# The bias stage of an attention and mixture-of-experts kernel gets its own division of PSUM

## The chip, the cores and the metric

One core of a Trainium2 chip runs the whole program. The metric is the device time of one execution in microseconds; lower is better. The kernel before takes 603.62 us, the median of three runs (601.79 to 604.7).

## The reference

An attention layer whose scores carry a computed bias, followed by a mixture of experts with one expert per token. B, H, S, D = 4, 8, 576, 64; the bias net has 32 hidden units; the experts have D = 512, F = 1024, E = 8.

```python
scores = scale * np.matmul(q, k.transpose(0, 1, 3, 2))
x = (psi_rel / psi_i)[..., None]             # 576 x 576 positions
h = np.maximum(x @ w1 + b1, 0.0)             # 32 hidden units
bias = h @ w2                                # one bias per head
attn = softmax(scores + bias.transpose(2, 0, 1)[None])
x = np.matmul(attn, v)                       # as 2304 tokens x 512
# each token goes to its best expert e:
out[mask] = gate * eom * (np.maximum(x[mask] @ w1[e], 0.0) @ w2[e])
```

## The kernel before, in words

The program is written out in a fixed order: each engine executes its instructions in the order in which the Python code emits them, and waits only on semaphores. It has three parts.

**The stage of the bias** (the loop `for r16 in range(36)`) builds the bias tables of all heads. A step, called a bias row here, covers 16 query positions. `emit_hid` writes four tiles of hidden units (128x576), each by VectorE (L725) or ScalarE (L723); the string `ON_ACT` has one digit for each row that says how many of the four ScalarE takes. `emit_bias` multiplies them with the second layer on TensorE (16 matmuls, L736) into a tile `pb` of two PSUM banks. ScalarE scales and copies it out (L740) into one of four staging rows `evh`, `evl`, and SyncE's queue sends the row to the bias table in SBUF (L746; in the last four rows L749, two DMAs each). A staging row is written again four bias rows later, when its DMA has landed. The hidden tiles are emitted two rows ahead and have three buffers.

Between the rows stands work of the first pairs of heads, placed by the table `BEGIN`: `l` is the six loads of keys and queries of pair 1 (`emit_load`), `v` the load of the values of pair 0 (`emit_load_v`), `k0` to `k2` and `K0` to `K2` are the transposes of keys and queries of pairs 0 and 1 (`emit_kq`: three transposes on TensorE, L809, a rounding copy by ScalarE, L812, called cast here, and the rest by VectorE, L814, called split here), and `s00`, `s10`, `s01`, `s11` are scores of pair 0, one head each (`emit_s`: TensorE L832, then VectorE adds the bias and finds the row's extreme, L844, then ScalarE's exponential, L849). What `BEGIN` names for a row starts on TensorE behind that row; its second half is emitted one row later, behind the next hidden tiles.

**The pairs of heads.** Behind the loop the pool of the stage is closed, GpSimd clears some tiles in its place (L976), and 16 pairs of heads follow in the order of the strings `FIRST`, `ORDER`, `LAST`, `END`. In them `s` is the products of a score tile, `m` its softmax, `t` transposes of the exponentials (L885, copied out at L889), `a` the product with the values (L917), `l` and `v` the loads of later pairs, `h` and `k` their transposes, `z` GpSimd's copies (L820) that build the query tile of the fifth block, which `s4` reads. A `+` means the next pair. On SyncE's queue the weights of the gate (L965) stand between the last bias rows and the loads of pair 2 (`l++`). The first `t` also makes GpSimd copy values (L802).

**The experts** follow and are bound by TensorE.

PSUM has eight banks. `ps_t` holds three places of one bank for all transposes, `ps_s` two places of two banks, which bias rows and scores share, and `ps_a` one bank for the product with the values.

Of the kernel before, what the change touches and what calls it, by code (L numbers as in the profile page):

```python
# [9 lines left out]
F32 = mybir.dt.float32  # L10
# [8 lines left out]
PSUM = bass.MemoryType.PSUM  # L19
# [30 lines left out]
)  # L50

FIRST = (
    "l++ t04d s2 t03a m2 t02d z t00a s3 m3 v+ s4 t01a m4 "
)

LAST = (
# [7 lines left out]
)  # L64

BEGIN = {
    3: "k0", 4: "k1", 5: "k2 l", 13: "K0", 16: "K1", 17: "s00", 20: "K2",
    22: "s10 s01", 32: "s11", 35: "v",
}

ON_ACT = "210210000111121212102110310010201111"

SLOT_WORK = (
# [8 lines left out]
def _first_row(r16):  # L82

    qb, g = divmod(r16, 8)
    return qb * 128 + (g if qb == 4 else g // 2 + 64 * (g % 2))
# [48 lines left out]
def attention_moe_kernel(  # L134
# [26 lines left out]
    xt_p = ctx.enter_context(tc.tile_pool(name="xt", bufs=3))  # L161
    x_p = ctx.enter_context(tc.tile_pool(name="x", bufs=2))
    st_p = ctx.enter_context(tc.tile_pool(name="st", bufs=4))
    ps_t = ctx.enter_context(tc.tile_pool(name="ps_t", bufs=3, space=PSUM))
    x_dram = dram.tile([NTOK, DM], F32, name="x_dram")

    n_kept = _WHERE["psi"][0]
# [14 lines left out]
    V.memset(gate, 0.0)  # L182

    def psum_t():
        return ps_t.tile([128, 512], F32, name="pt", tag="t")

    def over(ap, shape):
        return ap.rearrange("p (o e) -> p o e", o=1).to_broadcast(shape)
# [66 lines left out]
    def route_group(part):  # L255
# [4 lines left out]
        t0, nt = ((0, NTA), (NTA, NT - NTA))[part]  # L260
        ts = slice(t0, t0 + nt)
        pr = psum_t()
        rest = pm[:, t0 + 1:t0 + nt, :]
        n8 = nt * 8
# [119 lines left out]
        for u in range(nt // 5):  # L384
# [24 lines left out]
            yield  # L409
            yield  # L410
            pi = psum_t()
            for i in range(2):
                for t in range(5):
# [259 lines left out]
    with ExitStack() as actx:  # L673
        pool = lambda name, bufs, **kw: actx.enter_context(tc.tile_pool(name=name, bufs=bufs, **kw))
        kq = pool("kq", 1)
        ps_s = pool("ps_s", 2, space=PSUM)
        ps_a = pool("ps_a", 1, space=PSUM)


        bctx = ExitStack()  # L680
        e_p = pool("e", 1)
        e_all = [e_p.tile([128, 2, S], F32, name=f"e{i}") for i in range(4)]
        hb = bctx.enter_context(tc.tile_pool(name="hb", bufs=3))
# [30 lines left out]
        def emit_hid(r16):  # L714
            hid = hb.tile([128, 3, S], F32, name="hid", tag="hid")
            hid3 = xt_p.tile([128, S], F32, name="hid3", tag="xt0", bufs=4)
            for t in range(4):
# [3 lines left out]
                to = hid3 if t == 3 else hid[:, t, :]  # L721
                if t >= 4 - int(ON_ACT[r16]):
                    nc.scalar.activation(out=to, in_=src, func=ACTF.Relu, bias=bc[:, r:r + 1])  # L723
# [6 lines left out]

        def emit_bias(r16, hids):
            ev = evs[r16 // 2 % 2][:, r16 % 2, :]
            pb = ps_s.tile([128, 2, 512], F32, name="pb", tag="s")
            for c in range(2):
                for t in range(4):
                    nc.tensor.matmul(  # L736
                        pb[32 * t:32 * t + 32, c, 0:288], lhsT=w2f, rhs=hids[t][:, c * 288:c * 288 + 288],
                        start=True, stop=True,
                    )
            nc.scalar.activation(  # L740
                out=ev.rearrange("p (a j) -> p a j", a=2), in_=pb[:, :, 0:288], func=ACTF.Copy,
                scale=cinv[:, r16:r16 + 1],
            )
            p0 = _first_row(r16) % 128
            if r16 < 32:
                nc.sync.dma_start(out=bias[r16 // 8][p0:p0 + 61:4], in_=ev)  # L746
            else:
                for hl in range(2):
                    nc.sync.dma_start(  # L749
                        out=bias[4][hl * 64 + p0:hl * 64 + p0 + 61:4],  # L750
                        in_=ev.rearrange("(n t) j -> t n j", t=2)[hl]
                    )
# [71 lines left out]
        def products(b, pr, qb, heads, outs):  # L824

            high, low = (t[(b * NPAIR + pr) % 2] for t in (high2, low2))
            for c in range(2):
                for i, (t, keys) in enumerate(((0, high), (0, low), (1, high))):
                    qs = (high, low)[t]
                    for hl in heads:  # L830
                        p = slice(hl * 64, hl * 64 + 64) if qb < 4 else slice(0, 128)
                        nc.tensor.matmul(  # L832
                            outs[hl][:, c, 0:288],
                            lhsT=qs[p, S + 64 + qb * 128:S + 192 + qb * 128] if qb < 4 else q4[:, t, :],
                            rhs=keys[p, c * 288:c * 288 + 288], start=i == 0, stop=i == 2,
                        )
# [4 lines left out]
        def softmax_rows(e, ps, bias_ap, sum_ap):  # L841
            nm = st_p.tile([128, 1], F32, name="nm", tag="nm")
            n = e.shape[-1] // 2
            V.tensor_tensor_reduce(  # L844
                out=e.rearrange("p (a j) -> p a j", a=2), in0=ps[:, :, 0:n],
                in1=bias_ap.rearrange("p (a j) -> p a j", a=2),
                scale=-0.125, scalar=3.0e38, op0=ALU.add, op1=ALU.min, accum_out=nm,
            )
            nc.scalar.activation(out=e, in_=e, func=ACTF.Exp, scale=-1.0, bias=nm, accum_out=sum_ap)  # L849

        def emit_s(b, pr, qb, heads=(0, 1)):
            if b not in sums_t:
                sums_t[b] = st_p.tile([128, 4, H], F32, name="sums", tag="sums", bufs=2)
                sums4_t[b] = st_p.tile([128, NPAIR], F32, name="sums4", tag="sums4", bufs=2)
            if qb == 4:
                e = e_t[b, pr, 4] = e4[0]
                ps = ps_s.tile([128, 2, 512], F32, name="ps", tag="s")
                products(b, pr, qb, (0,), [ps])
                yield
                softmax_rows(e, ps, bias[4][:, pr, :], sums4_t[b][:, pr:pr + 1])  # L860
                return
            e_t[b, pr, qb] = e_all[qb]
            ps = {hl: ps_s.tile([128, 2, 512], F32, name="ps", tag="s") for hl in heads}
            products(b, pr, qb, heads, ps)
            yield
            for hl in heads:
                h = 2 * pr + hl
                softmax_rows(e_t[b, pr, qb][:, hl, :], ps[hl], bias[qb][:, h, :], sums_t[b][:, qb, h:h + 1])
# [69 lines left out]
        def finish(g):  # L938
            for _ in g:
                pass  # L940
# [19 lines left out]
        for g in halfway:  # L960
            finish(g)
        bctx.close()
        for hl in range(2):
            for i, w in enumerate((wg, wog)):
                nc.sync.dma_start(  # L965
                    out=wgb[hl * 64:hl * 64 + 64, :, hl * 16 + i * 8:hl * 16 + i * 8 + 8],
                    in_=w.rearrange("(a t d) e -> t d a e", t=2, d=64)[hl],
                )
# [23 lines left out]
        for n in range(len(pairs) + 1):  # L992
            for op in orders.get(n, ORDER).split():
                name = op.rstrip("+-")
# [24 lines left out]
                elif name[0] in "mh":  # L1019
                    finish(late.pop({"m": "s", "h": "k"}[name[0]] + name[1]))  # L1020
                    if name[0] == "m" and m == len(pairs) - 1:
# [3 lines left out]
                        if i == 2:  # L1025
                            t = biasp.tile([128, 4, 4, CH], F32R, name="x", tag="bias2")
# [22 lines left out]
    with ExitStack() as ctx:  # L1049
# [8 lines left out]
        hh, hl = ([t[:, i, :] for i in range(8)] for t in (hh_all, hl_all))  # L1058
# [190 lines left out]
```

## Time and profile before

| | |
|---|---|
| median of 3 runs | 603.62 us (601.79 to 604.7) |
| the profiled execution's own time | 601.0 us |
| its span, first to last instruction | 599.2 us |
| TensorE busy (matmul) | 565.7 us, 94% |
| VectorE busy | 395.6 us, 66% |
| ScalarE busy | 374.6 us, 63% |
| GpSimd busy | 106.2 us, 18% |
| mean granted clock of TensorE | 0.988 |

The profile records one execution, and its rows add up to the span. Times in a row are counted from the span's start. A busy TensorE has its matmuls pipelined, so a busy share alone says little; what counts is in which stretch it stands idle and for whom. An instruction's duration overlaps the next one's on the same engine by some 0.1 us, so the cost of one in a series is the distance of two starts.

### The profile page before, as it was taken

The numbers are of one execution on the slowest core, as the hardware profiler recorded it, in microseconds if no ns is written. First come the engines' busy times: TensorE is split into PE (matmuls) and PEld (weight loads), VectorE is DVE, ScalarE is ACT, GpSimd is POOL, SyncE is SP. The second block draws the span as 40 slices with busy tenths as digits, with TensorE's granted clock in tenths as the row PEclk, the third lists the DMA queues.
The fourth block names the chain that finished last, engine by engine and source line by source line (L and its number), as shares of the span: only waits on it lengthen the run. The fifth ranks groups of instructions, "written<-read, shape, count | busy, mean of one in ns | idle before, by whom it ended". The sixth has DMA issues, their size and how long they took to land.

```text
span 599.2 us, 13978 instructions
## 1 busy us (share of the span) xinstructions
PE 565.7 (94%) x5294; PEld 471.1 (79%) x5294; DVE 395.6 (66%) x936; ACT 374.6 (63%) x812; POOL 106.2 (18%) x220
## 2 busy tenths in 40 slices
PE   4888789999999999999999999999999999999993
PEld 2334467777778777877777769999999999999993
DVE  5978645665766668666789847676867765555521
ACT  5797767877777777777767764454545454555410
POOL 1000011000111110111103580030413223140302
PEclk9998989999999999999999999999999999999997
DMA  6965763321244331243322665675757475756521
GB/s 139 223 167 149 191 133 68 69 54 40 53 105 114 71 72 32 74 115 70 71 84 59 208 211 199 191 248 175 221 165 229 135 235 158 229 169 211 177 72 48
DMA packets 94998, 81.41 MB, mean 136 GB/s; under 512 B 71319, under 2 KB 71575, under 8 KB 94920
## 3 DMA queue, kind: packets, MB, share of 16 engines
q1 hardware_dynamic: 88932, 66.05, 40.7%
q0 software_dynamic: 3232, 9.64, 5.1%
q10 hardware_dynamic: 2756, 4.72, 2.2%
q8 instruction: 44, 0.72, 0.5%
q14 instruction: 34, 0.28, 0.1%
HBM read 60.34 MB, written 9.50 MB: 117 GB/s over the span
## 4 chain that ended last, share of the span: by engine, by line
PE 81%; issue 2%; DVE 1%; DMA 1%; POOL 1%; ACT 1%; SPq 1%; POOLq 0%
PE p L1101 16%; PE p L1122 16%; PE pa L917 14%; PE ps L832 12%; PE pt L885 11%; PE pt L809 3%; PE pt L897 2%; PE pt L656 2%; PE pt L1141 1%; PE pt L514 1%; PE pt L587 1%; SPq L749 1%; DMA vt<-in_v_dram 1%; DMA xg<-x_dram,gidx 1%; POOL out_dram L1066 0%
## 5 line engine op out<-in xcount | busy, mean ns | idle before, releaser
L844 DVE CUSTOM_DVE_ANT_0 e<-ps,bias 128x576 f32<-128x576 f32 x144 | 103.9, 754 | 57.2 <-PE ps L832 51.5
L849 ACT ACTIVATE e<-e,nm 128x576 f32<-128x576 f32 x144 | 111.1, 775 | 13.4 <-DVE nm L844 13.3
L1101 PE MATMUL p<-x,w 128*128 128x288 f32 x768 | 105.9, 297 | 0.0
L1101 PEld LDWEIGHTS p<-x,w 128*128 128x128 f32 x768 | 102.8, 188 | 0.5 <-issue 0.4
L889 ACT COPY et<-pt 128x512 f32<-128x512 f32 (+1 forms) x111 | 57.9, 557 | 36.2 <-PE pt L885 36.0
L885 PE MATMUL pt<-kept,e 128*128 128x128 f32 x576 | 79.6, 279 | 0.7 <-ACT et L889 0.4
L1122 PE MATMUL p<-hh,w2h 128*128 128x288 f32 x256 | 77.4, 302 | 0.0
L1122 PE MATMUL p<-hl,w2h 128*128 128x288 f32 x256 | 75.7, 296 | 0.1
L1122 PE MATMUL p<-hh,w2l 128*128 128x288 f32 x256 | 75.4, 295 | 0.0
L917 PE MATMUL pa<-et,vt 128*64 128x256 f32 (+1 forms) x640 | 73.2, 354 | 0.2 <-DVE xt L918 0.2
L885 PEld LDWEIGHTS pt<-kept,e 128*128 128x128 f32 x576 | 63.4, 141 | 10.6 <-issue 4.6
L736 PE MATMUL pb<-hid,w2blk 128*32 128x288 f32 x576 | 45.8, 437 | 16.7 <-DVE hid L725 7.6
L917 PEld LDWEIGHTS pa<-et,vt 128*64 128x64 f32 x640 | 42.6, 137 | 21.9 <-issue 7.3
L1066 POOL DMA_INDIRECT out_dram<-y,sidx x22 | 26.3, 1198 | 173.5 <-DVE y L1144 147.2
L1103 ACT ACTIVATE hh<-p 128x288 fp32r<-128x288 f32 x64 | 26.3, 411 | 45.7 <-PE p L1101 39.7
L725 DVE TENSOR_SCALAR hid<-e,early 128x576 f32<-128x576 f32 x110 | 48.4, 519 | 6.3 <-PE pb L736 2.9
L736 PEld LDWEIGHTS pb<-hid,w2blk 128*32 128x32 f32 x576 | 19.3, 115 | 39.6 <-DVE hid L725 10.0
L832 PE MATMUL ps<-qt 64*128 64x288 f32 x256 | 47.2, 347 | 2.0 <-DVE nm L844 1.7
L486 DVE TENSOR_TENSOR w2l<-w2r,w2h 128x1024 fp32r<-128x1024 f32 x32 | 39.3, 1227 | 14.3 <-ACT w2h L485 13.8
L1122 PEld LDWEIGHTS p<-hh,w2h 128*128 128x128 f32 x256 | 48.1, 188 | 0.6 <-issue 0.6
L1122 PEld LDWEIGHTS p<-hl,w2h 128*128 128x128 f32 x256 | 48.1, 188 | 0.3 <-DVE hl L1104 0.3
L1122 PEld LDWEIGHTS p<-hh,w2l 128*128 128x128 f32 x256 | 48.2, 188 | 0.0
(222 smaller groups left out, 959.2 us busy)
## 6 DMA issues: line engine op xcount, KB each, us to landing
w1r<-in_moe_w_dram SPq DMA_DIRECT2D x36, 512.0 KB, 3.6
w2r<-in_moe_w_dram SPq DMA_DIRECT2D x36, 512.0 KB, 4.1
bias<-evh SPq DMA_DIRECT2D x16, 288.0 KB, 3.6
bias<-evl SPq DMA_DIRECT2D x16, 288.0 KB, 3.6
vt<-in_v_dram SPq DMA_DIRECT2D x16, 288.0 KB, 3.4
nat<-in_k_dram SPq DMA_DIRECT2D x32, 128.0 KB, 2.9
nat<-in_q_dram SPq DMA_DIRECT2D x32, 128.0 KB, 2.5
x_dram<-x ACTq DMA_DIRECT2D x12, 256.0 KB, 2.3
```

Of the source, the lines that this page charges most:

```text
L486: V.tensor_tensor(out=lo, in0=src, in1=hi.bitcast(F32), op=ALU.subtract)
L725: V.tensor_scalar(out=to, in0=src, scalar1=bc[:, r:r + 1], scalar2=0.0, op0=ALU.add, op1=ALU.max,)
L736: nc.tensor.matmul(pb[32 * t:32 * t + 32, c, 0:288], lhsT=w2f, rhs=hids[t][:, c * 288:c * 288 + 288], start=True, stop=True,)
L832: nc.tensor.matmul(outs[hl][:, c, 0:288], lhsT=qs[p, S + 64 + qb * 128:S + 192 + qb * 128] if qb < 4 else q4[:, t, :], rhs=keys[p, c * 288 ...
L844: V.tensor_tensor_reduce(out=e.rearrange("p (a j) -> p a j", a=2), in0=ps[:, :, 0:n], in1=bias_ap.rearrange("p (a j) -> p a j", a=2), scal ...
L849: nc.scalar.activation(out=e, in_=e, func=ACTF.Exp, scale=-1.0, bias=nm, accum_out=sum_ap)
L885: nc.tensor.transpose(pt[:, n * 256 + j * 128:n * 256 + j * 128 + 128], es[j][:, (n0 + n) * 128:(n0 + n) * 128 + 128], ident,)
L889: copy(out=et[:, n0:n0 + nn, :].rearrange("p n s -> p (n s)"), in_=pt[:, 0:nn * 256])
L917: nc.tensor.matmul(pa[p:p + 64, 0:n], lhsT=values, rhs=weights, start=i == 0, stop=i == 4)
L1066: p = nc.gpsimd.indirect_dma_start(out=out, out_offset=bass.IndirectOffsetOnAxis(ap=idx, axis=0), in_=y[0:n], in_offset=None, bounds_check ...
L1101: nc.tensor.matmul(p1[:, 0:CH], lhsT=w[:, fs], rhs=x[:, c, :], start=n == 0, stop=n == 11)
L1122: nc.tensor.matmul(p2[:, 0:CH], lhsT=w[f // 2][:, f % 2, ds], rhs=x[f], start=n == 0, stop=n == 23)
```

## The change

The change divides PSUM anew for the stage of the bias alone: `ps_b`, three places of two banks for bias rows and scores, and `ps_k`, two places of one bank for the transposes. Both are closed with the stage, and only then are `ps_t`, `ps_s` and `ps_a` opened as before. `BEGIN` puts the loads, splits and scores behind other rows, `ON_ACT` gives ScalarE 36 of the 144 hidden tiles where it had 34, and `FIRST` has the steps of pair 0 in another order.

```diff
 FIRST = (
-    "l++ t04d s2 t03a m2 t02d z t00a s3 m3 v+ s4 t01a m4 "
+    "s2 m2 t04a l++ t00d s3 v+ z m3 s4 m4 t02a t01d t03d "
 )
 BEGIN = {
-    3: "k0", 4: "k1", 5: "k2 l", 13: "K0", 16: "K1", 17: "s00", 20: "K2",
-    22: "s10 s01", 32: "s11", 35: "v",
+    1: "l", 2: "k0 k2", 4: "k1", 5: "K0", 12: "s00", 19: "s10 s01 v", 32: "K2", 35: "s11 K1",
 }
-ON_ACT = "210210000111121212102110310010201111"
+ON_ACT = "041101121120201200221010102120102011"
...
-    ps_t = ctx.enter_context(tc.tile_pool(name="ps_t", bufs=3, space=PSUM))
+    ps_t = []
...
-        return ps_t.tile([128, 512], F32, name="pt", tag="t")
+        return ps_t[-1].tile([128, 512], F32, name="pt", tag="t")
...
-        ps_s = pool("ps_s", 2, space=PSUM)
-        ps_a = pool("ps_a", 1, space=PSUM)
         bctx = ExitStack()
+        ps_b = bctx.enter_context(tc.tile_pool(name="ps_b", bufs=3, space=PSUM))
+        ps_t.append(bctx.enter_context(tc.tile_pool(name="ps_k", bufs=2, space=PSUM)))
+        ps_s = [ps_b]
...
-            pb = ps_s.tile([128, 2, 512], F32, name="pb", tag="s")
+            pb = ps_b.tile([128, 2, 512], F32, name="pb", tag="s")
...
-            ps = {hl: ps_s.tile([128, 2, 512], F32, name="ps", tag="s") for hl in heads}
+            ps = {hl: ps_s[-1].tile([128, 2, 512], F32, name="ps", tag="s") for hl in heads}
...
         bctx.close()
+        ps_t.append(ctx.enter_context(tc.tile_pool(name="ps_t", bufs=3, space=PSUM)))
+        ps_s.append(pool("ps_s", 2, space=PSUM))
+        ps_a = pool("ps_a", 1, space=PSUM)
```

How the instructions move shows at three places. The first is TensorE at the end of the stage of the bias (`pb` is a bias row, `ps` a score, `pt` a transpose). Before:

```order
L736 MATMUL pb<-hid,w2blk 32x288 x3
L736 MATMUL pb<-hid_836,w2blk 32x288
L736 MATMUL pb<-hid,w2blk 32x288 x3
L736 MATMUL pb<-hid_836,w2blk 32x288
L885 MATMUL pt<-kept,e_136 128x128
L885 MATMUL pt<-kept,e_137 128x128
L832 MATMUL ps<-qt_118 128x288 x2
```

Now:

```order
L736 MATMUL pb<-hid,w2blk 32x288 x3
L736 MATMUL pb<-hid_821,w2blk 32x288
L832 MATMUL ps<-qt_115 128x288
L832 MATMUL ps<-qs_117,qt_115 128x288
L832 MATMUL ps<-qt_115,qs_117 128x288
L832 MATMUL ps<-qt_115 128x288
L832 MATMUL ps<-qs_117,qt_115 128x288
L832 MATMUL ps<-qt_115,qs_117 128x288
L809 MATMUL pt<-kept,nat 128x128 x3
L832 MATMUL ps<-qt_115 128x288 x2
```

The score `s11` (six matmuls) and the transposes `K1` (three) stand behind the last bias row now, before `s2` (the row with x2); before, `s11` stood three bias rows earlier.

The second is VectorE at the same place (`hid` is a hidden tile, `qs` a split, L844 with `e` a score). Before:

```order
L725 TENSOR_SCALAR hid<-e_139,early 128x576 x12
L844 ISA e_137,nm<-ps,bias_162 128x576
L844 ISA nm 128x1
L889 COPY et<-pt 128x256
L844 ISA e_138,nm<-ps,bias_163 128x576
```

Now:

```order
L725 TENSOR_SCALAR hid<-e_136,early 128x576 x6
L814 TENSOR_TENSOR qs_118<-pt,qt_116 128x384
L844 ISA e_134,nm<-ps,bias_159 128x576
L844 ISA nm 128x1
L814 TENSOR_TENSOR qs_118<-pt,qt_116 128x384
L844 ISA e_135,nm<-ps,bias_160 128x576
```

Two of the six splits (`K2`, `K1`) come behind the last hidden tile now.

The third is SyncE's queue early in the stage (`nat` is the loads of pair 1 that `l` issues). Before:

```order
L746 DMA bias_161<-evh 16x8x576 x2
L764 DMA nat<-in_k_dram 128x4x64 x2
L768 DMA nat<-in_k_dram 64x2x64
L764 DMA nat<-in_q_dram 128x4x64 x2
L768 DMA nat<-in_q_dram 64x2x64
L746 DMA bias_161<-evl 16x8x576 x2
```

Now:

```order
L768 DMA nat<-in_k_dram 64x2x64
L764 DMA nat<-in_q_dram 128x4x64 x2
L768 DMA nat<-in_q_dram 64x2x64
L746 DMA bias_158<-evl 16x8x576 x2
L746 DMA bias_158<-evh 16x8x576 x2
...
L746 DMA bias_160<-evl 16x8x576 x2
L774 DMA vt<-in_v_dram 128x9x64
L746 DMA bias_160<-evh 16x8x576 x2
```

Before, six bias rows (three lines `x2`, of which the last is shown) stand ahead of the loads; now two do. The load of the values `vt`, which stood behind all 36 bias rows, stands behind row 19.

## Rows read from the trace of the kernel before

**Rows 1.** The page's part 2: the span in 40 slices, TensorE and its clock.

```profile
PE   4888789999999999999999999999999999999993
...
PEclk9998989999999999999999999999999999999997
```

**Rows 2.** Timeline of PE: start, us, engine, line, operation, [idle before, releaser].

```profile
67.71 3.27 PE L736 MATMUL pb<-hid,w2blk 128*32 128x288 f32 x48 [2.32 <-DVE nm L844]
...
78.25 0.40 PE L832 MATMUL ps<-qt,q 128*128 128x288 f32 x1 [2.85 <-POOL q L820]
...
82.44 1.01 PE L809 MATMUL pt<-kept,nat 128*128 128x128 f32 x6
83.38 1.95 PE L917 MATMUL pa<-et,vt 128*64 128x256 f32 x16
```

**Rows 3.** Timeline of DVE in the stage of the bias.

```profile
31.29 1.38 DVE L725 TENSOR_SCALAR hid<-e,early 128x576 f32<-128x576 f32 x3 [1.06 <-ACT evh L740]
33.60 0.56 DVE L814 TENSOR_TENSOR qs<-pt,qt 128x384 fp32r<-128x384 f32 x1 [0.93 <-ACT qt L812]
...
41.90 4.39 DVE L725 TENSOR_SCALAR hid<-e,early 128x576 f32<-128x576 f32 x10 [1.28 <-PE pb L736]
...
50.30 0.76 DVE L844 CUSTOM_DVE_ANT_0 e<-ps,bias 128x576 f32<-128x576 f32 x1 [1.15 <-PE ps L832]
...
52.45 1.81 DVE L725 TENSOR_SCALAR hid<-e,early 128x576 f32<-128x576 f32 x4 [1.39 <-PE pb L736]
54.43 12.55 DVE L725 TENSOR_SCALAR hid<-e,early 128x576 f32<-128x576 f32 x29 [0.17 <-issue]
66.89 0.76 DVE L844 CUSTOM_DVE_ANT_0 e<-ps,bias 128x576 f32<-128x576 f32 x1
```

**Rows 4.** Timeline of ACT in the stage of the bias.

```profile
7.05 2.11 ACT L723 ACTIVATE hid<-e,early 128x576 f32<-128x576 f32 x3
...
27.26 0.74 ACT L740 ACTIVATE evl<-pb,early 128x576 f32<-128x576 f32 x1 [1.44 <-DMA bias<-evl]
...
54.47 0.74 ACT L740 ACTIVATE evh<-pb,early 128x576 f32<-128x576 f32 x1 [1.18 <-PE pb L736]
...
62.25 0.74 ACT L740 ACTIVATE evl<-pb,early 128x576 f32<-128x576 f32 x1
62.89 0.77 ACT L723 ACTIVATE hid<-e,early 128x576 f32<-128x576 f32 x1
...
64.84 0.74 ACT L740 ACTIVATE evh<-pb,early 128x576 f32<-128x576 f32 x1
```

**Rows 5.** Timeline of SyncE's queue: when it issues its DMAs.

```profile
19.30 1.16 SPq L764 DMA_DIRECT2D nat<-in_k_dram  x2
...
23.15 1.24 SPq L746 DMA_DIRECT2D bias<-evl  x2
...
71.03 2.47 SPq L749 DMA_DIRECT2D bias<-evl  x4
...
74.24 0.70 SPq L965 DMA_DIRECT2D wgb<-in_moe_w_gate_dram  x1
...
80.01 0.61 SPq L768 DMA_DIRECT2D nat<-in_q_dram  x1
```

**Rows 6.** The DMAs of the bias rows issued from 20 to 30 us: time to landing.

```profile
DMA to landing us min/median/max: 3.6/4.6/5.8
```

**Rows 7.** Windows: us, busy of PE, PEld, DVE, ACT, POOL, granted clock, DMA share, GB/s.

```profile
53.00:55.00 2.00, 2.00 (x20) 0.87 (x16) 1.83 (x5) 0.82 (x2) 0.00 (x0) 0.50 0.25 50
79.00:83.00 4.00, 4.00 (x24) 3.38 (x25) 1.27 (x3) 1.35 (x3) 0.00 (x0) 0.57 0.74 169
```

**Rows 8.** Timeline of PE's weight loads, four to each quarter of a bias row.

```profile
52.66 0.22 PEld L736 LDWEIGHTS pb<-hid,w2blk 128*32 128x32 f32 x4 [0.26 <-issue]
53.14 0.22 PEld L736 LDWEIGHTS pb<-hid,w2blk 128*32 128x32 f32 x4 [0.26 <-issue]
```

**Rows 9.** The chain that ended last, in order of time: the load of pair 0's values.

```profile
73.56 3.39 DMA vt<-in_v_dram
```

More of the change, by code (lines that the diff above doesn't have):

```diff
@@ L856, in emit_s @@
                 e = e_t[b, pr, 4] = e4[0]
-                ps = ps_s.tile([128, 2, 512], F32, name="ps", tag="s")
+                ps = ps_s[-1].tile([128, 2, 512], F32, name="ps", tag="s")
                 products(b, pr, qb, (0,), [ps])
```

## The prediction

> **What bounds the kernel now.** The page's slices say where to look: from the seventh of 40 on TensorE is busy at 9 tenths in every slice but the last, and in the first six it is not [rows 1]. So the time is the moment at which the pairs of heads begin to run at TensorE's pace, plus a rest that the change does not touch. I take as that moment the first product with the values (L917), which starts at 83.38 us [rows 2]. It is TensorE's own order that leads there: whatever makes that row start one microsecond earlier makes the kernel one microsecond shorter, as long as TensorE then finds its inputs.
>
> Next the timelines of the engines up to 83 us, read for the idle time in brackets. VectorE writes the last hidden tile of the bias at 54.43 + 12.55 = 66.98, and the next row starts at 66.89 [rows 3]. I call this moment H. From H to the first product 16.4 us pass.
>
> Until H, VectorE and ScalarE are the limit, not TensorE. 29 tiles in 12.55 us make 0.433 us a tile on VectorE [rows 3]; a tile costs ScalarE (2.11 - 0.77) / 2 = 0.67, and one copy of a bias row 0.64 (62.25 to 62.89) [rows 4]. A bias row with three tiles on VectorE costs it 1.30, and ScalarE with one tile and the copy 1.31. TensorE needs 3.27 / 3 = 1.09 [rows 2]. That 1.30 can be had is seen in the trace: from the copy at 54.47 to that at 64.84 are eight bias rows in 10.37 us, 1.30 each, with no wait for a DMA [rows 4]. Over the whole stage a row takes (66.98 - 7.05) / 36 = 1.66. The difference is waiting.
>
> VectorE's waits are of two kinds [rows 3]. At 41.90, 50.30 and 52.45 it waits for TensorE, 1.28 + 1.15 + 1.39 = 3.82 us: a score holds one of the two PSUM places until VectorE itself reads it, so TensorE works on bias rows with one place or none and the hidden tiles' buffers do not come free. At 31.29 and 33.60 it waits for ScalarE, 1.06 + 0.93 = 1.99: there ScalarE had stood 1.44 us for the DMA of a staging row [rows 4], whose issue came behind the six loads of `l` (SyncE's queue from 19.30 to 23.15 [rows 5]) and which landed late: 4.6 us in the middle and 5.8 at most [rows 6].
>
> **The change, part by part.**
>
> *Two tiles go to ScalarE* (34 to 36): VectorE -2 x 0.433 = -0.87. *Two splits go behind the last tile*: -2 x 0.56 less overlap, -1.0. These are work that VectorE does not have before H.
>
> *Three places.* A score now leaves two places to bias rows, and VectorE reads it while TensorE is on those two. I take the whole 3.82 away; between 0 and 3.82 is possible. TensorE is no new limit: 36 x 1.09 = 39 us and less than 10 us of scores and transposes lie in more than 50 us.
>
> *The loads of pair 1* stand behind two bias rows instead of six. The queue is busy for 3.85 us with them as before, only from about 13 us on, and the third bias row's DMA issues near 17. It lands 4.6 to 5.8 later, at 21.6 to 22.8, and ScalarE wants that staging row for the seventh bias row at about 20. So the wait of 1.4 us comes back at 1.6 to 2.8 us. VectorE is two rows ahead there and has one more PSUM place behind it, so I let it feel 1.0 of it in place of 1.99 (0 to 3.0).
>
> So H goes from 66.98 to 66.98 - 0.87 - 1.0 - 3.82 - 1.0 = 60.3. ScalarE is not later: 7.05 + 36 x (0.67 + 0.64) = 54.2, and six casts and three exponentials, none dearer than 0.77, make at most 61.1, when the last copy is due about 61.6 (below).
>
> *The end of the stage.* Before, TensorE had waited 2.32 us for VectorE to read `s11` and did three bias rows after H, to 67.71 + 3.27 = 70.98 [rows 2]. Now `s11` stands behind the last row, of which half is left at H: the last bias matmul ends at T = H + 0.6, its copy at H + 1.3.
>
> *The values.* GpSimd makes its copies for `s4` in order behind those of the values, whose load was issued behind the last bias row at 73.56 and landed 3.39 later [rows 9]; TensorE stood 2.85 us for GpSimd at 78.25 [rows 2], and from 79 to 83 the granted clock was 0.57 [rows 7], which costs (1 - 0.57) x 4 = 1.7 us. Now the values are there at half the stage. The clearing of tiles still waits for the last copy (H + 1.3), and under 3 us of GpSimd work brings its tile to H + 4, when TensorE reaches `s4` at about H + 7. Both 2.85 and 1.7 go.
>
> *TensorE's path then.* From 70.98 to the transposes of pair 2 at 82.44 are 11.5 us; less 2.85 and 1.7 they are 6.9. In front of them come `s11` and `K1`, 1.4 us, and `s2` waits for the split of `K1`, some 1.1 us, since it takes banks that the stage held. TensorE reaches the transposes of pair 2 at H + 0.6 + 1.4 + 1.1 + 6.9 = H + 10.0.
>
> *What is late next* is SyncE's queue. Those transposes need the last of the six loads `l++`, and these stand behind the last bias rows and the weights of the gate. Before, the queue was through the bias rows at 71.03 + 2.47 = 73.50, 2.5 behind the last bias matmul; from the first weight at 74.24 to the last load at 80.01 are 5.8; and it had landed by 82.44, 2.4 later [rows 2, 5]. Now: T + 2.5 + 5.8 + 2.4 = H + 11.3. That is later than TensorE's H + 10.0, so TensorE waits 1.3 us here, which it did not before. With 0.9 for the six transposes the first product starts at H + 12.2 = 72.5 instead of 83.38.
>
> **The sum** is -10.9 us: 6.7 before H, 4.2 behind it. Against the profiled execution's own time of 601.0 that is 590.1. This execution lies 2.6 below the median of 603.62, so I forecast **592.7**.
>
> The bounds: H is at best 59.3 (ScalarE's wait hidden) and at worst 66.98 - 1.87 + 1.0 = 66.1 (no stall goes, and the loads cost 3.0 where they cost 1.99). Behind H it is at best 10.9 (the queue is not late) and at worst 14 (the new wait is followed by low clock as at 79). That gives 590.4 to 600.3.
>
> **The rivals.**
>
> *A. The places do not matter.* If the engines are too evenly loaded, each wait for a cast or an exponential comes through, and VectorE keeps its 5.8 us of waits under other names. For it: both engines have at most some 1 us to spare at 1.30 a row. Against it: 1.30 was held for eight rows. H is then 65.1, the first product at 77.3, the time 597.5, with 594.5 to 602 around it.
>
> *B. The staging rows bind.* At 1.4 us a row, a DMA of a bias row has four rows, 5.6 us, for the copy (0.74), the issue and 3.6 to 4.6 of landing. For it: 5.8 was measured beside the loads [rows 6]. Against it: the eight rows at 1.30. Price: 1.5 to 4 us, 594 to 597.
>
> *C. TensorE's clock falls in the stage*, and this one is slower than before. In the stretch after the waits at 50 us the granted clock was 0.50, the lower level of 1.2 GHz [rows 7], and the loads of a quarter row came 0.48 apart [rows 8]: a bias row takes 1.92 us, not 1.09, and TensorE becomes the limit at 1.4 a row. Each such row costs 0.5 us against my forecast, so it decides from about 28 of the 36 rows on, with 592.7 + 28 x 0.5 = 606.7. All 36 and the scores and transposes at this level would give some 620. Against it: what came before was 1 to 2 us of TensorE standing idle, several times; and this is what the change takes away.
>
> On this rival the Trainium skill speaks against the change: in "TensorE: Matmul & The Clock Gate", section "A second HAM failure mode: psum-queue depth-cycling", it tells of a kernel that rotates through PSUM banks, whose TensorE idles briefly between groups so often that its clock goes to and fro between the levels. By that rule three places in rotation would give C, by the rows of this trace the forecast. The trace speaks for the rows: the kernel before rotates through two places with short idle times all through the stage, and the clock line [rows 1] shows only 8 to 9 tenths in it.
>
> **How the numbers follow.** The forecast with its neighbourhood (589 to 595): 0.64. A: 0.22, of which a third lies within 0.5% of the time before. B: 0.08. C: 0.06, nearly all slower. About 0.5%, 3 us, is what a measurement can tell from no change. Faster is then 0.64 + 0.15 + 0.08 = 0.87, the same 0.08, slower 0.05. The range takes in B and most of A above, and below the best bound with the runs' spread of about 2 us: 588.5 to 599.5.
>
> **What would show it.** Right: the last hidden tile on VectorE ends between 59 and 62; VectorE's rows of hidden tiles have no wait for TensorE over 0.5 us; ScalarE waits 1 to 3 us for a staging row's DMA near 20 us; TensorE has no wait for GpSimd at `s4`, but one of about 1 us for a load ahead of the transposes of pair 2; the first product starts at 72 to 73. Wrong: H at 64 or later (A), waits of ScalarE for DMAs throughout (B), granted clock of 0.5 over several slices (C), or a first product at 72 with a time above 597, which would mean that the rest of the kernel is not the same.

## The result, and the profile after

The changed kernel takes **593.41 us**, the median of four runs (592.74 to 593.86); beside it the kernel before took 604.1 (601.79 to 604.7, four runs). The ratio is 0.9829 with a 95% interval of 0.9800 to 0.9858: faster by 1.7%, beyond the 0.5% that can be told from no change. The forecast was 592.7 in a range of 588.5 to 599.5. The profiled execution of the changed kernel took 593.73 us, with a span of 591.9.

The page's part 2 answers to [rows 1]: TensorE is at 9 tenths from the second slice to the last but one, with a single 8, and no slice has a clock under 9 until the last.

```profile
PE   4999899999999999999999999999999999999993
...
PEclk9999999999999999999999999999999999999998
```

The timeline of DVE (start, us, engine, line, operation, [idle before, releaser]) answers to [rows 3].

```profile
26.60 3.96 DVE L725 TENSOR_SCALAR hid<-e,early 128x576 f32<-128x576 f32 x9 [0.34 <-ACT evh L740]
...
31.67 9.54 DVE L725 TENSOR_SCALAR hid<-e,early 128x576 f32<-128x576 f32 x22 [0.35 <-PE pb L736]
...
43.04 17.70 DVE L725 TENSOR_SCALAR hid<-e,early 128x576 f32<-128x576 f32 x41 [0.36 <-PE pb L736]
61.41 0.56 DVE L814 TENSOR_TENSOR qs<-pt,qt 128x384 fp32r<-128x384 f32 x1 [0.67 <-ACT qt L812]
64.28 0.76 DVE L844 CUSTOM_DVE_ANT_0 e<-ps,bias 128x576 f32<-128x576 f32 x1 [2.31 <-PE ps L832]
```

VectorE writes 41 tiles without a pause, and the last one ends at 43.04 + 17.70 = 60.74. That is H; it was 66.98. The three waits for TensorE of 1.15 to 1.39 us are gone; the largest left is 0.61, early in the stage. What replaced them shows on ACT, whose rows that wait 0.5 us or more for a DMA answer to [rows 4]:

```profile
22.36 0.74 ACT L740 ACTIVATE evl<-pb,early 128x576 f32<-128x576 f32 x1 [0.74 <-DMA bias<-evl]
...
55.00 0.74 ACT L740 ACTIVATE evh<-pb,early 128x576 f32<-128x576 f32 x1 [1.18 <-DMA bias<-evh]
56.39 0.74 ACT L740 ACTIVATE evh<-pb,early 128x576 f32<-128x576 f32 x1 [0.65 <-DMA bias<-evh]
...
63.85 0.74 ACT L740 ACTIVATE evl<-pb,early 128x576 f32<-128x576 f32 x1 [0.54 <-DMA bias<-evl]
```

ScalarE stands early in the stage as before, now at 22 us for 0.74 where it was 1.44 at 27, and now also at the end of the stage, where each wait delays a copy, then the PSUM place, then TensorE. The timeline of PE, to be read beside [rows 2]:

```profile
55.80 1.18 PE L736 MATMUL pb<-hid,w2blk 128*32 128x288 f32 x16 [0.71 <-ACT evh L740]
57.18 2.49 PE L736 MATMUL pb<-hid,w2blk 128*32 128x288 f32 x16 [0.21 <-ACT evh L740]
59.60 0.55 PE L809 MATMUL pt<-kept,nat 128*128 128x128 f32 x3
60.08 3.19 PE L736 MATMUL pb<-hid,w2blk 128*32 128x288 f32 x48
...
65.88 0.40 PE L832 MATMUL ps<-qt 64*128 64x288 f32 x2 [1.16 <-DVE qs L814]
...
70.35 0.37 PE L832 MATMUL ps<-qt,q 128*128 128x288 f32 x1 [0.83 <-DVE nm L844]
...
75.40 0.75 PE L809 MATMUL pt<-kept,nat 128*128 128x128 f32 x5 [1.47 <-DMA nat<-in_q_dram]
76.08 1.95 PE L917 MATMUL pa<-et,vt 128*64 128x256 f32 x16
```

At 60.08 three rows of bias (x48, 16 matmuls a row) are still to be done, and the last bias matmul ends at 60.08 + 3.19 = 63.27. I call this moment T. `s4` (70.35) has no wait for GpSimd any more; the transposes of pair 2 wait 1.47 us for the last load. SyncE's queue, as in [rows 5]:

```profile
64.55 2.47 SPq L749 DMA_DIRECT2D bias<-evl  x4
67.11 0.64 SPq L968 DMA_DIRECT2D wgb<-in_moe_w_gate_dram  x1
...
72.99 0.61 SPq L768 DMA_DIRECT2D nat<-in_q_dram  x1
```

The first product starts at 76.08 where it started at 83.38, 7.3 us earlier, and the spans differ by 599.2 - 591.9 = 7.3. So all of the difference between the two profiled executions lies ahead of the first product, as assumed. The medians differ by more, 10.7; the section on the prediction comes back to this. Beside the experiments e1 to e4 two of the 17 executions of the kernel before took 794.6 and 1095.36 us; they are in no median and no ratio here.

### The profile page after: what moved, and what is told of

It is laid out like the page before. It is cut to its first block, busy times and chain, and to the rows that moved or that the text cites. A ratio compares the mean times of both kernels' runs of the same rounds, so it can differ in the third digit from the quotient of the medians.

```text
span 591.9 us, 13980 instructions
## 1 busy us (share of the span) xinstructions
PE 567.2 (96%) x5294; PEld 473.7 (80%) x5294; DVE 395.7 (67%) x935; ACT 374.2 (63%) x813; POOL 106.1 (18%) x220
## 4 chain that ended last, share of the span: by engine, by line
PE 87%; ACT 3%; DMA 3%; DVE 2%; issue 2%; SPq 1%; POOL 0%; POOLq 0%; ACTq 0%; DVEq 0%
PE p L1104 17%; PE p L1125 16%; PE pa L917 14%; PE ps L832 12%; PE pt L885 11%; PE pb L736 4%; PE pt L809 3%; PE pt L897 2%; PE pt L655 2%; DMA bias<-evh 2%; PE pt L1144 1%; PE pt L513 1%; PE pt L586 1%; ACT evh L740 1%; ACT hid L723 1%
## 5 line engine op out<-in xcount | busy, mean ns | idle before, releaser
L844 DVE CUSTOM_DVE_ANT_0 e<-ps,bias 128x576 f32<-128x576 f32 x144 | 103.9, 753 | 55.2 <-PE ps L832 51.3
L917 PE MATMUL pa<-et,vt 128*64 128x256 f32 (+1 forms) x640 | 73.3, 354 | 0.2 <-DVE xt L918 0.2
L917 PEld LDWEIGHTS pa<-et,vt 128*64 128x64 f32 x640 | 42.9, 137 | 21.7 <-issue 7.3
L736 PE MATMUL pb<-hid,w2blk 128*32 128x288 f32 x576 | 49.5, 430 | 9.0 <-DVE hid L725 7.7
L736 PEld LDWEIGHTS pb<-hid,w2blk 128*32 128x32 f32 x576 | 22.8, 113 | 32.9 <-DVE hid L725 10.8
```

The costliest lines, as they stand in the source:

```text
L736: nc.tensor.matmul(pb[32 * t:32 * t + 32, c, 0:288], lhsT=w2f, rhs=hids[t][:, c * 288:c * 288 + 288], start=True, stop=True,)
L844: V.tensor_tensor_reduce(out=e.rearrange("p (a j) -> p a j", a=2), in0=ps[:, :, 0:n], in1=bias_ap.rearrange("p (a j) -> p a j", a=2), scal ...
L917: nc.tensor.matmul(pa[p:p + 64, 0:n], lhsT=values, rhs=weights, start=i == 0, stop=i == 4)
```

## The experiments

Each kernel was timed beside the kernel before on the same chip (604.1 for the change; 603.29 beside e1 to e4, 604.97 beside e5 to e8, 603.57 beside e9 to e12), so the ratios are what to compare. H is read from DVE's last group of hidden tiles, and "first product" is L917; both come from one trace of each kernel. Kernels whose text has one line more show line numbers that are higher by one.

| kernel | H | first product | median us | ratio, 95% interval |
|---|---|---|---|---|
| before | 66.98 | 83.38 | | 1 |
| e1: new places alone | 65.48 | 83.67 | 602.15 | 0.9978 (0.9955 to 1.0001) |
| e9: change, old `BEGIN` | 64.50 | 83.70 | 601.70 | 0.9965 (0.9950 to 0.9980) |
| e10: change, old `ON_ACT` | 63.53 | 78.68 | 596.44 | 0.9876 (0.9848 to 0.9904) |
| e2: change, two places | 62.70 | 76.57 | 594.63 | 0.9867 (0.9820 to 0.9914) |
| the change | 60.74 | 76.08 | 593.41 | 0.9829 (0.9800 to 0.9858) |
| the change again (e11) | 61.70 | 77.13 | 593.35 | 0.9822 (0.9798 to 0.9846) |
| e3: change, values late | 61.18 | 76.47 | 593.61 | 0.9830 (0.9797 to 0.9863) |
| e7: change, `s11` early | 61.39 | 77.58 | 594.91 | 0.9835 (0.9795 to 0.9874) |
| e8: change, old `FIRST` | 60.58 | 75.94 | 593.67 | 0.9831 (0.9791 to 0.9870) |
| e4: change, gate late | 60.20 | 73.91 | 592.53 | 0.9822 (0.9788 to 0.9856) |
| e5: change, six staging rows | 59.29 | 75.33 | 590.72 | 0.9769 (0.9742 to 0.9797) |
| e6: e5 and e4 together | 58.63 | 72.35 | 590.46 | 0.9769 (0.9740 to 0.9799) |
| e12: e6, `K1` one row earlier | 59.06 | 75.23 | 591.46 | 0.9788 (0.9764 to 0.9812) |

The changed kernel was traced twice, and H differs by 0.96 us between the two traces and the first product by 1.05. So a difference of 1 us or less between two rows of these columns cannot be told from none. What lies behind the first product is nearly the same in all traces: the span less the start of the first product is 515.6 to 516.3 us, in e1 517.0.

### Which part carries the gain: e1, e2, e9, e10

**e1** has the new division of PSUM and the old tables.

> The kernel before with the new division of PSUM alone: three places for bias rows and scores, two for transposes in the stage, tables as before. My theory: VectorE's three waits for TensorE (1.28 + 1.15 + 1.39 us) go, its last hidden tile ends about 63 instead of 66.98; the values still come late, so GpSimd still holds up s4; gain about 4 us of the change's 10, time about 600. Rival A (the places do not matter, the new places in the tables do it): within 1 us of the kernel before, last hidden tile at 66 to 67.

The whole division is worth 0.2%, at the edge of what can be told, and near rival A; H is 1.5 us earlier, where 4 had been expected. Its waits at the scores are still there, though three places were to take them away. All engines of e1, from 44 to 51 us:

```profile
44.60 1.80 DVE L726 TENSOR_SCALAR hid<-e,early 128x576 f32<-128x576 f32 x4
44.61 2.11 ACT L724 ACTIVATE hid<-e,early 128x576 f32<-128x576 f32 x3
...
46.31 0.75 DVE L845 CUSTOM_DVE_ANT_0 e<-ps,bias 128x576 f32<-128x576 f32 x1
46.61 0.74 ACT L741 ACTIVATE evl<-pb,early 128x576 f32<-128x576 f32 x1
...
47.13 0.40 PE L833 MATMUL ps<-qt 64*128 64x288 f32 x1 [1.78 <-DVE nm L845]
...
49.04 4.32 PE L737 MATMUL pb<-hid,w2blk 128*32 128x288 f32 x40 [0.86 <-DVE nm L845]
...
50.96 1.81 DVE L726 TENSOR_SCALAR hid<-e,early 128x576 f32<-128x576 f32 x4 [1.97 <-PE pb L737]
```

Just behind the first of the two scores ScalarE has three hidden tiles in a row, and its copy of an earlier bias row stands behind them, at 46.61; VectorE has four tiles ahead of its read of the score. TensorE stands 1.78 and 0.86 us, and then VectorE stands 1.97 for TensorE. The releaser of the second score is VectorE's read of the first; why that score needs it with three places I did not find out. The 1.5 us at H are lost again behind it: the last three bias rows take 4.81 us where they took 3.27, and the granted clock from 60 to 70 us is 0.83.

**e2** takes the third place away from the changed kernel.

```diff
-        ps_b = bctx.enter_context(tc.tile_pool(name="ps_b", bufs=3, space=PSUM))
+        ps_b = bctx.enter_context(tc.tile_pool(name="ps_b", bufs=2, space=PSUM))
```

> The changed kernel with two places for bias rows and scores instead of three, everything else as changed. My theory: the waits of VectorE for TensorE at the scores come back, 3 to 4 us, time about 597. Rival A: no difference, 593 to 594. A third reading: since the DMAs of the staging rows hold ScalarE up late in the stage of the changed kernel, a part of the loss is hidden behind them and only 1 to 2 us show.

In DVE's timeline the wait for TensorE behind the score `s00` is back, 1.28 us where the changed kernel has 0.35:

```profile
33.50 9.54 DVE L725 TENSOR_SCALAR hid<-e,early 128x576 f32<-128x576 f32 x22 [1.28 <-PE pb L736]
```

H is 1.96 us later than in the first trace of the changed kernel and 1.00 later than in the second. The time is later by 1.2 us by the medians and 2.3 by the ratios, as the third reading had it, but the intervals overlap. In this trace TensorE waits only 0.50 us for the last load of pair 2 where the changed kernel waits 1.47, so the queue hid a part.

**e9** and **e10** give the changed kernel back its old `BEGIN`, or its old `ON_ACT` (the lines of the diff above, one at a time).

> The changed kernel with the whole table BEGIN of the kernel before; its division of PSUM, ON_ACT and FIRST stay changed. Theory, BEGIN carries most of the gain: the two splits come back before the last hidden tile (1.0 us), the loads of pair 1 collide with staging rows again (1.0 us more wait), the scores stand in rows 17 to 32 against an ON_ACT made for others (1 to 3 us), and GpSimd waits for values again (2 to 3 us at s4): last hidden tile at 63.5 to 65.5, 597 to 600. Rival, ON_ACT carries it: 594 to 596.

> The changed kernel with the string ON_ACT of the kernel before; its division of PSUM, BEGIN and FIRST stay changed. VectorE has two tiles more (0.87 us). Theory, that string and BEGIN belong together: with rows of three tiles on ScalarE beside its casts and exponentials VectorE waits for ScalarE or TensorE again, 2 to 4 us before the last hidden tile, which then ends at 63 to 65.5: 595.5 to 598. Rival, only the two tiles count and the queue's wait hides part of them: 593.4 to 594.5.

With the old `BEGIN` nearly all of the gain is gone, more than I expected: 601.7. In its trace VectorE reads scores late again, and TensorE waits twice for that; at `s4` (77.13) it waits for GpSimd (PE):

```profile
48.75 13.33 PE L737 MATMUL pb<-hid,w2blk 128*32 128x288 f32 x160 [2.80 <-DVE nm L845]
...
65.22 4.81 PE L737 MATMUL pb<-hid,w2blk 128*32 128x288 f32 x48 [2.14 <-DVE nm L845]
...
77.13 0.61 PE L833 MATMUL ps<-qt,q 128*128 128x288 f32 x1 [2.46 <-POOL q L821]
```

From H to the first product this kernel takes 83.70 - 64.50 = 19.2 us, the changed one 76.08 - 60.74 = 15.3. So `BEGIN` is worth some 3.8 us before H and as much behind it. Behind H the trace shows three things that the changed kernel does not have: the wait of 2.14 for the read of `s11`, the last three bias rows in 4.81 us instead of 3.19, and the wait of 2.46 at `s4`, with a granted clock of 0.50 from 76 to 82 us. With the old `ON_ACT` the loss is 0.54%, as expected in size, though its wait is not the one I named: the largest is for a staging row.

```profile
56.63 0.74 ACT L740 ACTIVATE evl<-pb,early 128x576 f32<-128x576 f32 x1 [3.13 <-DMA bias<-evl]
```

What follows from the four: the places alone are worth little (0.2%), and so are all other parts without `BEGIN` (0.35%). With `BEGIN` most of the gain of 1.7% stays, without the new `ON_ACT` (1.2%) as without the third place (1.3%). So `BEGIN` carries most of it; whether it would do so alone was not tested. The third place gives 1 to 2 us at H on top, and what it gives in time is not clear of the noise.

### The order behind the stage: e8, e7

**e8** has the old `FIRST`; **e7** moves one score.

```diff
-    1: "l", 2: "k0 k2", 4: "k1", 5: "K0", 12: "s00", 19: "s10 s01 v", 32: "K2", 35: "s11 K1",
+    1: "l", 2: "k0 k2", 4: "k1", 5: "K0", 12: "s00", 19: "s10 s01 v", 32: "K2 s11", 35: "K1",
```

> The changed kernel with the order of pair 0's steps of the kernel before (transposes t04d ahead of s2, z late). Theory, behind the stage the loads of pair 2 end last whatever stands between, so with the same issues on the queue the first product moves by under 1 us: 593 to 594.5. Rival, the order is a part of the gain, since GpSimd's copies for s4 come late again and TensorE waits 2 to 3 us for them at s4: 595 to 597.

> The changed kernel with the score s11 back behind row 32 in place of 35; the transposes K1 stay at 35. Theory, that its place behind the last row took VectorE's read of it (0.76) and TensorE's wait for that read (2.32 before) out of the way: the last hidden tile ends 0.8 to 1.5 us later, the stretch behind the stage is shorter by the six matmuls of the score (about 0.8), and since the queue's wait hides part of it, the time is 593.5 to 595.5. Rival, the place of this score is worth nothing, as with the values: within 0.5 of 593.4.

Both ratios are those of the changed kernel within their intervals. The order of `FIRST` is worth nothing that can be told here; the last load of pair 2 still ends last (TensorE waits 1.28 us for it in e8). In e7 H lies between those of the two traces of the changed kernel, T is H + 3.5 instead of H + 2.5, and the wait for the load is longer, 1.69, but by its ratio the place of `s11` alone cannot be told from nothing. So it was not shown that this score's place is the part of `BEGIN` behind H; how that part divides among its entries was not separated.

### The values' load: e3

```diff
-    1: "l", 2: "k0 k2", 4: "k1", 5: "K0", 12: "s00", 19: "s10 s01 v", 32: "K2", 35: "s11 K1",
+    1: "l", 2: "k0 k2", 4: "k1", 5: "K0", 12: "s00", 19: "s10 s01", 32: "K2", 35: "s11 K1 v",
```

> The changed kernel with the load of the values behind the last bias row, as before. If the term for the values adds by itself: +2.9 to +4.5 us, about 597. My theory by the changed kernel's profile: the transposes of pair 2 wait for the queue anyway (1.47 us), so most of it is hidden; s4 comes about 1.9 us later and the loads of pair 2 0.7 us later, together +0.7 to +2 us, about 595, with GpSimd waiting for the values' DMA until about 70.5.

The time is the same, below both figures expected. Rows of e3 on DVE and PE:

```profile
43.49 17.69 DVE L725 TENSOR_SCALAR hid<-e,early 128x576 f32<-128x576 f32 x41 [0.22 <-PE pb L736]
...
59.09 3.31 PE L736 MATMUL pb<-hid,w2blk 128*32 128x288 f32 x48
...
70.70 0.59 PE L832 MATMUL ps<-qt,q 128*128 128x288 f32 x1 [2.02 <-POOL q L820]
```

TensorE waits for GpSimd again at `s4`, 2.02 us where it waits 0.83 for VectorE in the changed kernel, and its clock falls: 0.69 from 70 to 72 us and 0.50 from 72 to 74, an estimated 1.7 us lost. Yet the first product is only 0.39 later. Two things pay for it. The wait of 1.47 for the last load is gone; and T comes 0.9 us earlier (62.40). T is H + 1.2 here; it is H + 2.5 or 2.6 in the five traces with the early load, three places, four staging rows and `s11` behind the last row (the change twice, e4, e8, e10). The reason stands in the DMA engines. For 42 to 50 us, first the changed kernel, where the load is issued at 42.29 (packets, then the bias rows' KB and time to landing):

```profile
DMA packets 1906, 1.82 MB, mean 227 GB/s; under 512 B 1246, under 2 KB 1246, under 8 KB 1906
...
bias<-evh SPq DMA_DIRECT2D x3, 288.0 KB, 5.6
```

and the same stretch of e3:

```profile
DMA packets 837, 1.71 MB, mean 213 GB/s; under 512 B 96, under 2 KB 96, under 8 KB 837
...
bias<-evh SPq DMA_DIRECT2D x3, 288.0 KB, 3.9
```

The values come as 1150 packets of 256 B, as many bytes as one bias row (288 KB), while the bias rows alone need 288 KB in each 1.30 us, 227 GB/s. The windows of the changed kernel (us, busy of PE, PEld, DVE, ACT, POOL, granted clock, DMA share, GB/s) show no room for it, and the first of them in e3 (the last line) has a share of 0.69:

```profile
42.00:47.00 5.00, 5.00 (x82) 2.75 (x74) 4.64 (x12) 4.99 (x11) 0.00 (x0) 1.00 1.07 229
47.00:52.00 5.00, 5.00 (x62) 2.50 (x60) 5.00 (x12) 4.69 (x8) 0.00 (x0) 1.00 1.06 229
...
42.00:47.00 5.00, 5.00 (x79) 2.83 (x79) 4.78 (x13) 4.90 (x10) 0.00 (x0) 1.00 0.69 184
```

So the rows behind the load land 5.6 us after their issue and not 3.9, and the four staging rows come free too late: ScalarE's waits at 55.00 and 56.39. By these two traces the early load saves some 2.9 us at `s4` and in the clock behind it, and costs 2.3 through the staging rows and the queue; in the time the two cannot be told apart.

On this the Trainium skill says, in "DMA: Bandwidth & Descriptors", section "Where 436 GB/s comes from", that for transfers inside SBUF the ports' ceiling of 435 GB/s binds. By these traces the DMA engines are full far earlier, for rows of 2304 B: windows of 5 us with a share of 1.0 and more show 224 to 251 GB/s in the traces of the changed kernel, e3 and e5.

### The gate's weights: e4

The four loads of `wgb` are issued behind all steps of `FIRST`, and so behind the loads of pair 2.

```diff
-        for hl in range(2):
-            for i, w in enumerate((wg, wog)):
-                nc.sync.dma_start(
...
+            if n == 1:
+                for hl in range(2):
+                    for i, w in enumerate((wg, wog)):
+                        nc.sync.dma_start(
```

> The changed kernel with the four DMAs of the gate's weights issued behind those of pair 2 instead of ahead of them. My theory (SyncE's queue is what comes late after the stage): the loads of pair 2 issue 2.7 us earlier, the wait of 1.47 us ahead of their transposes goes, the first product with the values starts at about 74.6 instead of 76.08, time 1.3 to 1.5 us below the changed kernel's, about 592. Rival (TensorE's own path is as long): within 0.3 us of the changed kernel.

The wait is gone (PE: L809 at 73.11 has no bracket), and the first product comes 2.2 us earlier, of which 0.5 is an earlier T. The median is 0.9 lower, the ratio 0.9822: the direction is as expected, but by the intervals it can't be told from the changed kernel's, which in its second measurement has the same ratio.

### Six staging rows: e5, e6, e12

```diff
+        evs.append(hb.tile([128, 2, S], F32, name="evm", bufs=1))
...
-            ev = evs[r16 // 2 % 2][:, r16 % 2, :]
+            ev = evs[r16 // 2 % 3][:, r16 % 2, :]
```

> The changed kernel with six staging rows in place of four; nothing else. In its trace ScalarE waits late in the stage for the DMA of a staging row three times (1.18, 0.65, 0.54 us), and the last bias matmul ends 2.5 us behind the last hidden tile where I had forecast 0.6. Theory, the number of rows binds: these waits go, the last bias matmul ends about 1 us behind the last hidden tile, the last load of pair 2 is issued 1 to 1.5 us earlier, the first product starts near 75, and the time falls by 0.7 to 1.5 us, to 592 to 592.7. Rival, the DMA engines' rate binds (a bias row of 295 KB each 1.30 us is 227 GB/s, and the windows show 224 to 226 with a share above 1): ScalarE's waits go all the same, but the rows queue up in the engines, so the issues or the landing of the last rows and of the loads behind them are as late as before, and the time stays within 0.4 us of 593.4.

> Six staging rows and the weights of the gate behind the loads of pair 2: both edits together. The gate's alone gave 592.53, with no wait for a load ahead of the transposes of pair 2. By theory, TensorE's own path sets the end then, and an earlier last bias row is worth its full amount: 591.3 to 592. Rival, the rate of the DMA engines binds: 592.2 to 592.8, as with the gate alone.

e5 is faster than the change by some 3 us (2.7 by the medians, 3.2 to 3.6 by the ratios), more than expected, and its interval lies just below both of the change's. Rows of e5 on DVE, PE and SyncE's queue:

```profile
41.60 17.69 DVE L726 TENSOR_SCALAR hid<-e,early 128x576 f32<-128x576 f32 x41
...
56.74 3.78 PE L737 MATMUL pb<-hid,w2blk 128*32 128x288 f32 x48
...
60.48 3.00 SPq L750 DMA_DIRECT2D bias<-evm  x4
...
69.44 0.61 SPq L769 DMA_DIRECT2D nat<-in_q_dram  x1
```

No ACT row of the stage waits for a DMA any more. H is 41.60 + 17.69 = 59.29, T = 60.52 = H + 1.2, and the queue is through the bias rows at 63.48 = T + 3.0, with the last load issued 3.55 us earlier than in the changed kernel. The DMA engines are as full as they are there from 42 to 52 us (1.05 and 237 GB/s from 55 to 60), so the rival fell: it was the number of rows that bound, since with six a row may land late. e6 is below what both its readings expected, but gains nothing on e5 that can be told; in e5 no wait for the load is left that its second edit could take away. Its profiled execution, the earliest of all, has

```profile
71.54 0.88 PE L810 MATMUL pt<-kept,nat 128*128 128x128 f32 x6
72.35 1.95 PE L918 MATMUL pa<-et,vt 128*64 128x256 f32 x16
```

and e5's first product stands 3 us later. Its windows show TensorE's clock:

```profile
66.00:68.00 2.00, 0.78 (x11) 0.54 (x9) 1.75 (x4) 1.26 (x4) 1.28 (x7) 0.95 0.38 62
68.00:70.00 2.00, 1.67 (x6) 1.58 (x7) 0.29 (x2) 1.27 (x4) 0.71 (x3) 0.50 0.68 151
70.00:72.00 2.00, 2.00 (x12) 1.98 (x11) 0.77 (x3) 0.82 (x3) 0.00 (x0) 0.50 0.67 154
```

TensorE did 0.78 us of work in two, and then ran at 0.50, 1.2 GHz, until 74: 6 us at half speed, 3 us lost. This execution took 593.44, the longest of e5's seven. e6's trace has low clock too, but less (0.77, 0.50 and 0.88 in the windows of 2 us from 62 to 68). Whether six rows have a part in this was not tested.

> Six staging rows and the gate's weights behind the loads of pair 2 (which gave 590.46), and the transposes K1 one bias row earlier, so that their split is done when s2 starts. Theory, behind the stage TensorE's own path sets the end now, so its wait of 1.16 us for that split is worth most of itself: 589.3 to 590.2. Rival, TensorE finds the time again at s4 (GpSimd's copies, 0.94 us in that trace) or at VectorE's reads of the scores: 590.2 to 590.8.

```diff
-    1: "l", 2: "k0 k2", 4: "k1", 5: "K0", 12: "s00", 19: "s10 s01 v", 32: "K2", 35: "s11 K1",
+    1: "l", 2: "k0 k2", 4: "k1", 5: "K0", 12: "s00", 19: "s10 s01 v", 32: "K2", 34: "K1", 35: "s11",
```

A miss for both: 591.46, not told from e6 by the intervals. The wait for the split of `K1` is gone, but in e12's trace TensorE waits 0.95 us for VectorE in the same place and 2.05 at `s4`, and the clock falls from 68 to 74 us as in e5.

### The change again: e11

> The changed kernel as it is, measured beside the others of this call, and a second look at its trace. Expected 593 to 594, and the same two places in the trace: ScalarE's waits for staging rows between 53 and 57 us, and TensorE's wait for the last load of pair 2 near 75.

593.35, as before. H differs by 1.0 us between the two traces of the same kernel, through ScalarE's early waits for staging rows (0.74 us in one; 0.38 and 1.36 in the other). The waits of 1.08 and 0.59 at 56 and 57 us are there, and T is H + 2.5 again. Behind T the two traces differ: here the clock falls, which it does not in the first,

```profile
68.00:70.00 2.00, 2.00 (x11) 1.65 (x11) 1.84 (x5) 1.07 (x3) 0.03 (x1) 0.50 0.60 159
```

and TensorE comes later to the transposes of pair 2, so that its wait for the last load is 0.67 and not 1.47.

## Why the prediction held, and which of its terms did not

**What held.** The time is set by the moment of the first product, and the rest of the kernel is unchanged: 7.3 us there, 7.3 in the span, and 515.6 to 517.0 us behind it in every trace. The new wait for the last load came (1.3 said, 1.47 measured), as did `s2`'s wait for the split of `K1` (1.1 said, 1.16 measured) and ScalarE's early wait for a staging row, shorter than said in the first trace (1.6 to 2.8 said; 0.74, and 1.74 in e11). The wait for GpSimd and the low clock behind it went; e3, with the load back in its old place, has both again. H of 59.3 as the best case, "ScalarE's wait hidden", is near what six rows show: 59.29, 58.63 and 59.06 in e5, e6 and e12.

Rival C did not come. By the rule quoted there, three places in rotation would make the clock swing; the windows of the changed kernel from 20 to 66 us, the end of the stage and more, have a granted clock of 1.00 in both traces.

**H: a near hit, in part by luck.** H fell by 6.2 where 6.7 was said, but not by the terms as they were sized. VectorE's waits for TensorE before H add up to 4.0 us before and 1.5 after: the 3.82 us for the places brought 2.5. Its waits for ScalarE add up to 2.5 before and 0.7 after: the 1.0 us for the loads brought 1.8. In e11's trace, where the waits for ScalarE are 2.0, H is 61.70, 1.4 late. The sign "no wait for TensorE over 0.5 us" was missed by a wait of 0.61.

**What was mis-sized.** The forecast's first product was 72.5, measured 76.08, outside the 72 to 73 given as the sign of being right:

| step | forecast | measured | late by |
|---|---|---|---|
| H | 60.3 | 60.74 | 0.4 |
| last bias matmul, T | H + 0.6 | H + 2.5 | 1.9 |
| queue through the bias rows | T + 2.5 | T + 3.75 | 1.25 |
| from there to the first product | 9.1 | 9.06 | 0 |

These are the step "The end of the stage" and the 2.5 us of "What is late next". I took it that half a bias row is left at H. In fact 2.5 us of the x48 line were left, 2.4 bias rows, since ScalarE had stood for staging rows at 55.00 and 56.39, and the copy at 63.85, on which the queue's last issues hang, stood once more. e5 takes these waits away and gives T = H + 1.2 and T + 3.0, so some 2.05 of the 3.15 are the staging rows, and the rest my optimism. e3 keeps four rows and takes the load out of them, and it has T = H + 1.2 as well. This is rival B in small: it was put at 1.5 to 4 us, but as another case than the likeliest, with the argument that eight rows had gone by at 1.30 us without a wait. They did so without a load between them. I had costed the move of the values only on GpSimd; the packets of its load in the middle of rows that fill the engines were the other half, and by e3 the two cancel within what can be told, some 2 us.

**The term of 3.82 us for the three places** was credited to the wrong part of the change. The three waits went, but e1 shows 1.5 us at H from the places alone and e2 1.0 to 2.0 from the third place among the new tables; e9 and e10 show that most of the rest needs `BEGIN`, and some of it `ON_ACT`. "A score leaves two places to bias rows" was not enough in e1, where ScalarE has three tiles ahead of a copy; that these tiles are the cause was not tested alone. Rival A, that the waits come through under other names, is near what happens to the division without the tables.

**Two errors met.** In profiled executions the change gave 7.3 us where the sum said 10.9. The median still came within 0.7 us of the forecast, by luck: I put the 2.6 us between the profiled execution of before and its median on top. They do not belong to the changed kernel: its profiled execution lies 0.3 above its median. The kernel before varies by its clock. Of its eleven runs beside e5 the fastest, 601.59 us, had a mean granted clock of 0.990, the slowest, 606.72, one of 0.980; 1% of 600 us is 6, and they differ by 5.1. The nine runs of the changed kernel have 0.991 to 0.996 and 592.74 to 594.92. So besides the 7.3 us the change takes away low clock that the profiled execution of before (0.988) had less of than most. The medians differ by 2.9 to 3.4 us more than the profiled executions; by the median clocks, 0.982 in those eleven runs and 0.994 in the nine, an estimated 2.4 of it are clock (0.006 less than the profiled execution before, 0.002 less after). Part of that low clock lies in the stage itself: from 50 to 60 us the clock is 0.83 before, 0.86 in e1, 0.92 in e9, and 1.00 in the changed kernel. I had counted the low clock from 79 to 83 us of that one execution (1.7) and no more.

## What to carry to other kernels

A load that is moved away from a wait is issued somewhere: look at the DMA share of the stretch that it enters, and at how many buffers wait for landings there, before calling the move free. When one execution is the base of a sum, look at how the other runs of that kernel spread and whether their clock goes with it; a gain in idle time can be worth more in the median than in the trace. And more places in PSUM need not pay by themselves; look at what the engine that empties them does in between: the same division gave 0.2% with one table of tiles and was part of 1.7% with another, most of which two places gave as well.

## What the runs showed that I had not expected

The DMA engines are full, with a share of 1.0 and above, at 224 to 251 GB/s in windows of 5 us for SBUF rows of 2304 B, and time to landing was 5.6 us in such a stretch and 3.9 in the same stretch with less to move (e3); two more staging rows then gave some 3 us at the same rate.

Whether the clock falls behind a gap is not set by the gap alone in these traces. e5 did 0.78 us of work from 66 to 68 and then ran at 0.50; the changed kernel did 0.60 from 74 to 76 and went on at 1.00:

```profile
74.00:76.00 2.00, 0.60 (x5) 0.54 (x5) 1.26 (x4) 0.08 (x1) 0.00 (x0) 1.00 0.76 173
```

The clock falls behind the stage in the traces of e3, e5, e6, e11 and e12, and not in those of the change, e2, e4, e7, e8 and e10; e11 is the changed kernel itself. What decides it was not tested, and it cost up to 3 us of one execution.
